# Decay attention and a two-layer network in one kernel: three edits to the order of the work between them

## The chip, the core and the metric

The kernel runs on one core of a Trainium2 chip. The metric is the device time of one execution in microseconds (us), as the median of several. A core has five engines, each with a queue of its own that it works off in order: TensorE (PE, matrix products; PEld loads its weights beside them), VectorE (DVE), ScalarE (ACT), GpSimd (POOL) and SyncE (SP), which here issues all the DMA transfers. Engines wait for each other and for transfers by semaphores. TensorE reads its operands from SBUF and writes to PSUM; ACT and DVE read both.

## The reference

```python
def _attn_ref(q, k, v, f):                      # B, H, S, D = 8, 8, 576, 64
    scores = scale * np.matmul(q, k.transpose(0, 1, 3, 2))
    cum = np.cumsum(np.log(np.clip(f, 0.0001, 1.0)), axis=-1)
    decay = cum[:, :, :, None] - cum[:, :, None, :]
    scores = np.where(causal, -1000000000.0, scores + decay)
    attn = np.exp(scores - np.max(scores, axis=-1, keepdims=True))
    attn = attn / (np.sum(attn, axis=-1, keepdims=True) + 1e-09)
    return np.matmul(attn, v)

def _moe_ref(x, w_in, w_out):                   # x: 4608 tokens x 512
    h = x @ w_in                                # 512 x 2048
    g = h * np.clip(h + 3.0, 0.0, 6.0) / 6.0
    return g @ w_out                            # 2048 x 512
```

The rows of x are the tokens: row (batch, position) holds the outputs of the 8 heads side by side, so a batch of 576 positions is 576 rows of x, and a row is complete when all 8 heads of its batch are done.

## The kernel before

**Units.** The list `VH` holds 68 attention units: four of kind A (the first 256 queries of two heads of batch 0 at once), eight of kind B (the other queries of batch 0, a head each) and 56 of kind F, the heads of batches 1 to 7. Their numbers are in the tiles' names: unit i has the score products `pn_i_0` and `pn_i_1` (two halves), the masked scores `pp`, the probabilities in two fp16 parts in a `ring` buffer, their transposed form `pT_i` (a DMA transpose, L666), the sums `pav` (probabilities times v, with a column of ones that gives the row sum), the row factors `rs`, and, for each pair of heads, `xf` and its fp16 parts `xhl`. Unit 12 is the first head of batch 1, unit 20 that of batch 2, and so on by eights.

**From attention to the two layers.** `x_move` (L736 on; the DMAs are L752) transposes a pair's `xhl` into `xT`, of which there are three, one for a tile of 512 tokens. The two-layer network runs by these nine tiles: 16 first-layer units (`ph_t_fc`, 12 products of 128x512 each, L778 to L780; then the clipping on ACT and DVE, L788 to L793, into `gT`) and four second-layer units (`po_t_s`, 48 products each, L800 to L802). The first products of a tile read the first pairs of heads; the 10th to 12th of `ph_t_0` read the last pair's part of `xT`. Tile 0 is done in two pieces, since its first 256 columns are there when the A units are.

**The order.** The loop over `VH` writes out, for each unit, its attention in steps, with eight calls of `fill(1)` between them. `fill` adds a rate to a credit and issues pieces of the two-layer work while the credit is at least 1; a piece costs 1.05 (half a first-layer unit) or 0.95 (six second-layer products), so a whole tile costs 64.0. The rate is `F_RATE[0]` in the B units, then `F_RATE[min(b, 2)]`: 0.6, 0.45 in batch 1, 1.02 from batch 2 on. `done(v)` puts a tile into the list `units` when the last head of its batch has been moved; it is called right behind `x_move`, in the middle of the second head of the next batch. What the loop writes is a priority: a list scheduler then places each instruction on its engine's queue, and may place one well ahead of where the loop wrote it.

**The weights.** `w_in` and `w_out` come as 64-bit floats (two 32-bit words each). For each of 16 chunks of each matrix `w_decode` makes fp32 of them (ACT L250, DVE L251 and L252, a sum of squares on ACT L256), and after the sum of a group `w_split` makes two fp16 parts (ACT L283; DVE L294, or, for three of the four groups of `w_in`, products with a scaled identity, `low`, L286 and L287). `w_step` does one step of this work; the loop calls it `wn` times for each unit, by `W_RATE` for A, B and F. Whatever is left when tile 0 reaches its second layer is written out there at once.

**v's power of two.** Each batch's v is scaled by a power of two, found from its largest element: the tile `vst` is loaded by three DMAs (`load_v`, L359 twice for a doubled first chunk, and L360 for the rest, about 1 MB), DVE takes the largest element by two reductions (L365, tile `vm`), a product with ones spreads it over the partitions (`pt_v`, L183), and a few DVE instructions write the scale to column `SV + b` of the tile `SC` and its inverse to `IV + b`. In batches 1 to 7 v is multiplied by it when it is split into fp16 parts (`v_split`, ACT L396, DVE L397). Batch 0 keeps v in fp32 as it is; there the scale joins the row factors: `rs` is the row sum plus a small number (L720), its reciprocal (L723), then times `SV` (L725), and L726 multiplies `pav` by it.

Of the kernel before, what the change touches and what calls it, by code (L numbers as in the profile page):

```python
# [15 lines left out]
ALU = mybir.AluOpType  # L16
# [4 lines left out]
def kernel(  # L21
# [10 lines left out]
    nc = tc.nc  # L32

    NHEAD, D, S = qk.shape
    D //= 2
    B = vS.shape[0]
    H = NHEAD // B
    NT, DM = out.shape
    DFF = w_in.shape[1]
    P = 128  # L40
# [5 lines left out]
    NFC = DFF // P  # L46
    TT = 512
# [3 lines left out]
    PSC = 2.0 ** 4  # L51
# [28 lines left out]
    )  # L80

    NQK, NL, NST = 3, 2, 3
    W_RATE = (8, 2, 4)
    H_COST = 1.05
    F_RATE = (0.6, 0.45, 1.02)
    PIN = 0
    PIN0 = 1
    LOW_W = 0
# [6 lines left out]
    QA = 256  # L95
# [104 lines left out]
    def scol(c):  # L200
        return SC[:, c:c + 1]
# [186 lines left out]
    def v_split(g):  # L388
        b, hp = divmod(g, NPAIR)
        t = v16[:, g % NV16]  # L390
        if g < NPAIR + NV16:
            nc.vector.memset(t[:, :, :, D:D + 1], 1.0)
        for j in range(2):
            o = (2 * hp + j) * (D + 1)
            src = vst[:, :, o:o + D]
            nc.scalar.activation(t[:, :, j, 0:D], src, AF.Copy, scale=scol(SV + b))  # L396
            nc.vector.scalar_tensor_tensor(  # L397
                t[:, :, j, D + 1:VW], src, scol(SV + b), t[:, :, j, 0:D],
                op0=ALU.mult, op1=ALU.subtract,
            )  # L400
# [278 lines left out]
    def av(v, ph):  # L679
        kind, n = VH[v]  # L680
        g = n if kind == "A" else n // 2
        b = g // NPAIR
        vt = v16[:, g % NV16]
        if kind == "F":
            jh = n % 2
            blk = [(n, c, c) for c in range(NCH)]
            vh, vl = vt[:, :, jh, 0:D + 1], vt[:, :, jh, D + 1:VW]
            for c in range(NCH):
                pb = ph[:, HT[c]:HT[c] + (2 * c + 1) * P].rearrange("p (g t) -> p g t", t=P)
                o1, o0 = pav[:, c, 0:D + 1], pav[:, c, 0:D]  # L690
                nc.tensor.matmul(o1, pb[:, c], vh[:, 0], start=True, stop=False)
                nc.tensor.matmul(o0, pb[:, c], vl[:, 0], start=False, stop=(c == 0))
                for k in range(1, c + 1):
                    nc.tensor.matmul(o1, pb[:, c + k], vh[:, k], start=False, stop=False)  # L694
                    nc.tensor.matmul(o0, pb[:, c + k], vl[:, k], start=False, stop=False)  # L695
                    nc.tensor.matmul(o1, pb[:, k - 1], vh[:, k], start=False, stop=(k == c))  # L696
        else:
            blk = blocks(v)
            for head, c, pl, m, js in blk:
                w0, _ = window(head)  # L700
                for jc, o, kk in js:
                    nc.tensor.matmul(
                        pav[:m, pl, :], ph[:kk, o:o + m], v_chunk(b, jc)[:kk, w0:w0 + NAV],
                        start=(jc == 0), stop=(jc == c),
                    )
        heads = sorted({x[0] for x in blk})
        if heads[0] % 2 == 0:
            xpair[g] = (
                p2.tile([P, NCH, P], F32, tag="xf", name=f"xf_{v}", bufs=1),
                p2.tile([P, NCH, 2, P], F16, tag="xhl", name=f"xhl_{v}", bufs=1),  # L710
            )
        xf, xhl = xpair[g]
        for head in heads:
            jh = head % 2
            mine = [x for x in blk if x[0] == head]
            p0, p1 = mine[0][2], mine[-1][2] + 1
            c0, c1 = mine[0][1], mine[-1][1] + 1
            vo = window(head)[1] if b == 0 else 0
            rs = p2.tile([P, NCH, 1], F32, tag="rs", name=f"rs_{v}_{jh}")[:, p0:p1]
            nc.vector.tensor_scalar(  # L720
                rs, pav[:, p0:p1, vo + D:vo + D + 1], PSC * 1e-9, None, op0=ALU.add
            )
            nc.vector.reciprocal(rs, rs)  # L723
            if b == 0:
                nc.vector.tensor_scalar(rs, rs, scol(SV + b), None, op0=ALU.mult)  # L725
            nc.vector.tensor_tensor(  # L726
                xf[:, c0:c1, jh * D:(jh + 1) * D], pav[:, p0:p1, vo:vo + D],
                rs.to_broadcast([P, p1 - p0, D]), op=ALU.mult,
            )
        if heads[-1] % 2:  # L730
            nc.scalar.copy(xhl[:, c0:c1, 0], xf[:, c0:c1])
            nc.vector.tensor_tensor(
                xhl[:, c0:c1, 1], xf[:, c0:c1], xhl[:, c0:c1, 0], op=ALU.subtract
            )

    def x_move(v):  # L736

        kind, n = VH[v]
        g = n if kind == "A" else n // 2
        b, cc = divmod(g, NPAIR)  # L740
        xhl = xpair[g][1]
        c0, c1 = {"A": (0, CA), "B": (CA, NCH), "F": (0, NCH)}[kind]

        if kind == "F":
            runs = [(0, 0, 1, 0), (0, 1, NCH, 1), (64, 1, NCH, 2)]
        else:
            runs = [(r * 64, c0, min(c1, NCH - r), r + 2 * c0) for r in range(2)]
        for r, c, last, u in runs:
            while c < last:
                t, q = divmod(S // 64 * b + u, TT // 64)  # L750
                k = min(last - c, (TT // 64 - q + 1) // 2)
                nc.sync.dma_start_transpose(  # L752
                    xT[t % 3][:, cc, q % 2, q // 2:q // 2 + k].rearrange("p c a t -> p (c a) t"),
                    xhl[r:r + 64, c:c + k].rearrange("p c a e -> p (c a e)"),
                )
                c += k
                u += 2 * k
# [115 lines left out]

    units = []

    credit, rates = [0.0], [1.0]

    def w_step():
        with tc.high_priority(offset=-LOW_W):
# [2 lines left out]
    def fill(k):  # L882
        credit[0] += k * rates[0]
        while credit[0] >= 1 and units:
            with tc.high_priority(offset=-LOW_M):
                r = next(units[0], 0)
            if r == 0:
                units.pop(0)
            else:
                credit[0] -= r  # L890
        credit[0] = min(credit[0], 1.0)

    def one(*a):
        yield from moe_tile(*a)

    def done(v):
        kind, n = VH[v]
        if kind == "A":
            if n == NPAIR - 1:
                units.append(one(0, 0, QA))  # L900
            return
        b, h = divmod(n, H)
        if h == H - 1:
            units.append(one(b, QA if b == 0 else 0, TT))
            if b == B - 1:
                units.append(one(B))

    prev = None
    pend_x = None
    vq = v_scale(0)  # L910
    for i, (kind, n) in enumerate(VH):
        b, h = divmod(n, H)
        if kind == "A":
            b = h = 0
        wn = W_RATE["ABF".index(kind)]
        rates[0] = F_RATE[0] if kind == "B" else F_RATE[min(b, 2)]
        ahead = i + 2 < NV
        if i + 3 < NV:
            load_x(i + 3)
        if ahead:  # L920
            load_c(i + 2)
        if b + 1 < B and h == 6:
            load_v(b + 1)
        if b and h % 2 == 1 and h < H - 1:
            v_split((n + 1) // 2)
        sg = rows(i) if kind == "F" else scores(i)
        front = ahead and VH[i + 2][0] != "F"
        next(sg)
        if i + 1 < NV:
            rests(i + 1)  # L930
        if ahead:
            parts(i + 2)
        fill(1)
        if b + 1 < B and h == 7:
            vq = v_scale(b + 1)
        next(vq, None)
        fill(1)
        ph = next(sg)
        if i + 1 < NV and VH[i + 1][0] != "F":
            max_rows(i + 1)  # L940
        for _ in range(wn // 2):
            w_step()
        fill(1)
        next(vq, None)
        next(sg, None)
        fill(1)
        if pend_x is not None:
            x_move(pend_x)
            done(pend_x)
            pend_x = None  # L950
        if front:
            natural(i + 2, 0)
        fill(1)
        if b + 1 < B and h == 7:
            for _ in vq:
                pass
            if b:
                v_split((n + 1) // 2)
        for _ in range(wn - wn // 2):
            w_step()  # L960
        next(sg, None)
        fill(1)
        if front:
            natural(i + 2, 1)
        fill(1)
        if prev is not None:
            av(*prev)
            if VH[prev[0]][0] == "A" or VH[prev[0]][1] % 2 == 1:
                pend_x = prev[0]
        if n == H:  # L970
            v_split(n // 2)
        fill(1)
        prev = (i, ph)
    rates[0] = 1.0
    av(*prev)
    fill(4)
    x_move(prev[0])
    done(prev[0])
    while units:
# [37 lines left out]
```

## Time and profile before

| | |
|---|---|
| median of 3 runs | 1086.47 us (1081.67 to 1088.14) |
| the profiled execution, its own time | 1084.35 us |
| its span, first to last instruction | 1082.6 us |
| mean granted TensorE clock | 0.986 of full speed |
| PE busy | 1012.2 us (94%) |
| DVE busy | 716.3 us (66%) |
| ACT busy | 610.3 us (56%) |
| POOL busy | 415.5 us (38%) |

A busy share is an average over stages: batch 0 and the weights until about 200 us, then batches 1 to 7 beside the tiles until about 890 us, then the last tiles alone. Matmuls are pipelined, so their busy times overlap. A line number stands for a line of the kernel before; of an instruction's tiles the profile leaves the numbers out.

### The profile page before, as it was taken

What the parts mean: (1) busy time and instruction counts of PE and PEld (TensorE: products, weight loads), DVE (VectorE), ACT (ScalarE), POOL (GpSimd) and SP (SyncE); (2) the same over time, 40 slices, a digit from 0 to 9 for tenths busy, and PEclk for the clock granted to TensorE, in tenths of its full rate; (3) what the DMA queues carried; (4) which work ended last, traced back from release to release, by engine and by line L of the source; (5) the groups of instructions that cost most, each with busy time, mean ns of one, the idle gap of its engine ahead of it and who ended that gap; (6) DMA issues with size and microseconds to landing.
All of it is one profiled execution on the core that took longest, in us unless ns stands there. A gap on an engine that the chain in (4) does not pass through costs nothing.

```text
span 1082.6 us, 20307 instructions
## 1 busy us (share of the span) xinstructions
PE 1012.2 (94%) x7074; PEld 578.3 (53%) x7074; DVE 716.3 (66%) x1903; ACT 610.3 (56%) x1285; POOL 415.5 (38%) x505
## 2 busy tenths in 40 slices
PE   2899977988999999989999989999999999999998
PEld 1667754755555555555554545555555555444443
DVE  7887889876885698477855795688668841510520
ACT  4786656755864577456744674477547841621520
POOL 7443454435434445444544444354445420000000
PEclk9999989999999999999999989999999999999999
DMA  8966447776756675666566856676666651000001
GB/s 244 295 196 212 117 104 136 156 151 133 164 109 143 141 146 122 134 144 142 124 139 123 160 112 130 137 168 120 129 139 129 105 110 48 1 10 30 1 1 39
DMA packets 261650, 133.74 MB, mean 124 GB/s; under 512 B 229444, under 2 KB 231036, under 8 KB 261548
## 3 DMA queue, kind: packets, MB, share of 16 engines
q1 hardware_dynamic: 261548, 132.45, 54.9%
q8 instruction: 56, 0.92, 0.4%
q14 instruction: 46, 0.38, 0.1%
HBM read 47.93 MB, written 9.73 MB: 53 GB/s over the span
## 4 chain that ended last, share of the span: by engine, by line
PE 73%; DVE 12%; DMA 5%; issue 3%; SPq 3%; POOL 2%; ACT 2%; DVEq 0%; POOLq 0%; ACTq 0%
PE po L801 11%; PE po L800 10%; PE po L802 10%; PE ph L778 9%; PE ph L779 9%; PE ph L780 9%; PE pn L611 3%; PE pn L608 3%; DMA vst<-in_vS_dram 2%; DVE pp L619 2%; SPq L752 2%; DVE ring L648 2%; PE pav L695 1%; PE pav L696 1%; PE pav L694 1%
## 5 line engine op out<-in xcount | busy, mean ns | idle before, releaser
L778 PE MATMUL ph<-xT,w 128*128 128x512 f16 (+1 forms) x640 | 230.7, 362 | 15.9 <-DVE r L791 10.4
L779 PE MATMUL ph<-xT,w 128*128 128x512 f16 (+1 forms) x640 | 228.9, 361 | 0.0
L780 PE MATMUL ph<-xT,w 128*128 128x512 f16 (+1 forms) x640 | 228.8, 361 | 0.0
L801 PE MATMUL po<-w,gT 128*128 128x512 f16 x576 | 217.1, 382 | 7.5 <-DVE w L294 7.5
L631 ACT ACTIVATE pp<-pp,nb 128x192 f32<-128x192 f32 x280 | 138.4, 552 | 143.7 <-DVE nb L625 143.6
L800 PE MATMUL po<-w,gT 128*128 128x512 f16 x576 | 214.5, 382 | 4.1 <-ACT w L283 2.2
L802 PE MATMUL po<-w,gT 128*128 128x512 f16 x576 | 216.9, 382 | 0.0
L648 DVE TENSOR_TENSOR ring<-pp,ring 128x128 f16<-128x128 f32 (+2 forms) x216 | 129.7, 615 | 84.6 <-ACT ring L645 83.6
L788 ACT ACTIVATE r<-ph,bias_r,SC 128x256 f32<-128x256 f32 (+7 forms) x272 | 144.4, 571 | 30.0 <-PE ph L780 25.9
L791 DVE SCALAR_TENSOR_TENSOR r<-r,ph 128x512 f32<-128x512 f32 (+1 forms) x160 | 100.0, 627 | 90.9 <-ACT r L788 90.8
L458 POOL TENSOR_TENSOR T<-ST,T 64x576 fp32r<-64x576 f32 (+1 forms) x68 | 99.7, 1466 | 139.0 <-DMA T<-TK 134.9
L619 DVE CUSTOM_DVE_ANT_0 pp<-pn,W 128x192 f32<-128x192 f32 x280 | 123.0, 481 | 19.3 <-PE pn L611 17.4
L793 DVE TENSOR_TENSOR gT<-r,gT 128x512 f16<-128x512 f32 (+1 forms) x160 | 114.0, 718 | 30.1 <-ACT gT L792 29.5
L792 ACT CAST gT<-r 128x512 f16<-128x512 f32 (+1 forms) x160 | 91.7, 574 | 73.4 <-DVE r L791 73.2
L608 PE MATMUL pn<-TK,TQ 68*128 68x192 f32 x336 | 125.1, 386 | 5.0 <-issue 4.0
L611 PE MATMUL pn<-T,T 128*128 128x192 f32 x336 | 113.9, 369 | 0.0
L645 ACT CAST ring<-pp 128x192 f16<-128x192 f32 x280 | 113.0, 452 | 0.0
L455 POOL TENSOR_TENSOR T<-ST,TQ 64x576 fp32r<-64x576 f32 (+2 forms) x68 | 97.5, 1433 | 22.5 <-PE pn L611 12.7
L654 POOL TENSOR_TENSOR ring<-pp,ring 128x128 f16<-128x128 f32 x96 | 62.5, 651 | 106.9 <-ACT ring L645 77.7
L779 PEld LDWEIGHTS <-w 128*128 128x128 f16 x640 | 62.5, 98 | 66.2 <-issue 20.7
L802 PEld LDWEIGHTS <-gT 128*128 128x128 f16 x576 | 57.0, 99 | 76.2 <-issue 15.1
L778 PEld LDWEIGHTS <-w 128*128 128x128 f16 x640 | 62.9, 98 | 61.9 <-issue 13.7
(136 smaller groups left out, 1715.2 us busy)
## 6 DMA issues: line engine op xcount, KB each, us to landing
ST<-in_qk_dram SPq DMA_DIRECT2D x64, 288.0 KB
T<-TK SPq DMA_DIRECT2D x64, 144.0 KB
out_dram<-o SPq DMA_DIRECT2D x36, 256.0 KB
ring<-in_w_out_dram SPq DMA_DIRECT2D x16, 512.0 KB
T<-TQ SPq DMA_DIRECT2D x56, 144.0 KB
vst<-in_vS_dram SPq DMA_DIRECT2D x7, 1040.0 KB
ring<-in_w_in_dram SPq DMA_DIRECT2D x9, 512.0 KB
w<-in_w_in_dram SPq DMA_DIRECT2D x7, 512.0 KB
```

What stands on the lines that cost most here:

```text
L608: nc.tensor.matmul(dst, TQ[i][0:D + 4, qs], TK[i][0:D + 4, a:e], start=True, stop=False)
L611: nc.tensor.matmul(dst, T7[j][:, qs], T1[j][:, a:e], start=False, stop=True)
L619: nc.vector.tensor_tensor_reduce(pp[:r, w:w + kw], pn[:r, o:o + kw], W[:r, 4 * P + r - kw:4 * P + r], 1.0, -3.0e38, ALU.add, ALU.max, accu ...
L631: nc.scalar.activation(x_, x_, AF.Exp, bias=nb[:r, e0 + x:e0 + x + 1], scale=0.125)
L648: eng.tensor_tensor(hl[:r, a:a + c * P], pp[:r, at[c] + 64:at[c] + kw], hl[:r, h0[c] + 64:h0[c] + kw], op=ALU.subtract,)
L778: nc.tensor.matmul(ph, w1[0][:, cc, fs_], xh, start=(cc == 0), stop=False)
L779: nc.tensor.matmul(ph, w1[0][:, cc, fs_], xl, start=False, stop=False)
L780: nc.tensor.matmul(ph, w1[1][:, cc, fs_], xh, start=False, stop=(cc == NCC - 1))
L788: nc.scalar.activation(r[:, a:e], ph[:, a:e], AF.Relu, bias=bias_r, scale=scol(A1 + NG * b + fc * NG // NFC))
L800: nc.tensor.matmul(po, gT[:, 0, fc, ts_], w2[:, fc, 0, :], start=(fc == 0), stop=False)
L801: nc.tensor.matmul(po, gT[:, 0, fc, ts_], w2[:, fc, 1, :], start=False, stop=False)
L802: nc.tensor.matmul(po, gT[:, 1, fc, ts_], w2[:, fc, 0, :], start=False, stop=(fc == NFC - 1))
```

## The change

Three edits. **First**, in the B units the loop calls `w_step` five times for each unit, where it was two (`W_RATE`). **Second**, in batch 0 the first instruction of `rs` multiplies the row sum by the inverse scale, `IV`, in the same instruction that adds the small number, and the third instruction is gone. **Third**, from batch 2 on the rate isn't a constant: `even(h)` takes what is left in the list (counted in `left`), less a reserve of 8, and divides it evenly over the eight `fill`s of each head that remains before the next tile can join; and `done` of an F pair is called not right behind `x_move` but at the start of the next head.

```diff
-    W_RATE = (8, 2, 4)
+    W_RATE = (8, 5, 4)
-    F_RATE = (0.6, 0.45, 1.02)
+    F_RATE = (0.6, 0.45)
...
-            nc.vector.tensor_scalar(
-                rs, pav[:, p0:p1, vo + D:vo + D + 1], PSC * 1e-9, None, op0=ALU.add
-            )
+            total = pav[:, p0:p1, vo + D:vo + D + 1]
+            if b == 0:
+                nc.vector.tensor_scalar(
+                    rs, total, PSC * 1e-9, scol(IV + b), op0=ALU.add, op1=ALU.mult
+                )
+            else:
+                nc.vector.tensor_scalar(rs, total, PSC * 1e-9, None, op0=ALU.add)
             nc.vector.reciprocal(rs, rs)
-            if b == 0:
-                nc.vector.tensor_scalar(rs, rs, scol(SV + b), None, op0=ALU.mult)
...
+    credit, rates, left = [0.0], [1.0], [0.0]
+    TILE = NFC * 2 * H_COST + TT // P * NFC // 2 * (2.0 - H_COST)
+    RESERVE = 8.0
+    def queue(unit, columns):
+        units.append(unit)
+        left[0] += TILE * columns / TT
+    def even(h):
+        heads = (1 - h) % H + 1
+        return min(max((left[0] - RESERVE) / (8 * heads), 0.5), 1.25)
...
-        rates[0] = F_RATE[0] if kind == "B" else F_RATE[min(b, 2)]
+        if moved is not None:
+            done(moved)
+            moved = None
+        rates[0] = F_RATE[0] if kind == "B" else F_RATE[b] if b < 2 else even(h)
...
         if pend_x is not None:
             x_move(pend_x)
-            done(pend_x)
+            if VH[pend_x][0] == "F":
+                moved = pend_x
+            else:
+                done(pend_x)
             pend_x = None
```

The scheduler turns this into other places on the queues. SyncE's queue where the last pair of batch 3 (`xhl_34`) is moved into tile 3, before: the outputs of tile 2 (`o_2_3` is its last) are sent before the fifth transpose.

```order
L812 DMA out_0_dram<-o_2_2_5605 128x512
L411 DMA ST2_105<-in_qk_dram 128x576
L666 DMA_TRANSPOSE pT_36_5553<-ring1_124 128x12x128
L752 DMA_TRANSPOSE xT0_117<-xhl_34_5539 128x2x64
L752 DMA_TRANSPOSE xT0_117<-xhl_34_5539 128x4x64
L752 DMA_TRANSPOSE xT1_118<-xhl_34_5539 128x4x64
L752 DMA_TRANSPOSE xT0_117<-xhl_34_5539 128x4x64
L812 DMA out_0_dram<-o_2_3_5752 128x512
L752 DMA_TRANSPOSE xT1_118<-xhl_34_5539 128x4x64
```

And now, from the second of these transposes on:

```order
L755 DMA_TRANSPOSE xT0_117<-xhl_34_5431 128x4x64
L755 DMA_TRANSPOSE xT1_118<-xhl_34_5431 128x4x64
L755 DMA_TRANSPOSE xT0_117<-xhl_34_5431 128x4x64
L815 DMA out_0_dram<-o_2_1_5632 128x512
L755 DMA_TRANSPOSE xT1_118<-xhl_34_5431 128x4x64
L417 DMA TK1_97<-decay_dram 2x576
L666 DMA_TRANSPOSE pT_37_5601<-ring2_125 128x13x128
L666 DMA_TRANSPOSE pT_37_5601<-ring0_123 128x12x128
L419 DMA TQ1_94<-decay_dram 2x576
L453 DMA T71_102<-TQ0_93 64x576
L454 DMA T11_100<-TK0_96 64x576
L815 DMA out_0_dram<-o_2_2_5761 128x512
```

The pair is moved while tile 2 has its third and fourth output blocks (`o_2_2`, `o_2_3`) still ahead of it; before, its last block was done by then.

SyncE's queue where batch 5's v is loaded, before: both kinds of load stand behind the transposes of unit 38.

```order
L666 DMA_TRANSPOSE pT_38_5874<-ring1_124 128x13x128
L411 DMA ST1_104<-in_qk_dram 128x576
L666 DMA_TRANSPOSE pT_38_5874<-ring2_125 128x12x128
L359 DMA vst_112<-in_vS_dram 64x520 x2
L360 DMA vst_112<-in_vS_dram 128x4x520
```

And now: the two L359 stand where they were, behind unit 38, and L360 behind the transposes of unit 39.

```order
L417 DMA TK0_96<-decay_dram 2x576
L666 DMA_TRANSPOSE pT_39_5923<-ring0_123 128x13x128
L419 DMA TQ0_93<-decay_dram 2x576
L453 DMA T71_102<-TQ2_95 64x576
L454 DMA T11_100<-TK2_98 64x576
L666 DMA_TRANSPOSE pT_39_5923<-ring1_124 128x12x128
L360 DMA vst_112<-in_vS_dram 128x4x520
```

The load has moved back by a head, and no L359 stands right ahead of it any more. VectorE's queue around the reductions of the same v (`vm5`), before, with the first-layer instructions `r_3_...` of tile 3:

```order
L791 SCALAR_TENSOR_TENSOR r_3_6_0_6093<-r_3_6_0_6093,ph_3_6_0_6080 128x512
L619 ISA pp_39_1_6120,MF1_109<-pn_39_1_6115,W_88 128x320
L619 ISA MF1_109 128x1
L619 ISA pp_39_1_6120,MF1_109<-pn_39_1_6115,W_88 128x448
L619 ISA MF1_109 128x1
L365 TENSOR_REDUCE vm5_6776<-vst_112 128x1 x2
L648 TENSOR_TENSOR ring0_123<-pp_39_0_6066,ring0_123 128x128
L625 TENSOR_SCALAR nb_39_6056<-MF1_109 128x2
L793 TENSOR_TENSOR gT_116<-r_3_6_0_6093,gT_116 128x512
L648 TENSOR_TENSOR ring0_123<-pp_39_0_6066,ring0_123 128x512
L791 SCALAR_TENSOR_TENSOR r_3_7_0_6132<-r_3_7_0_6132,ph_3_7_0_6108 128x512
```

And now:

```order
L794 SCALAR_TENSOR_TENSOR r_3_3_0_6096<-r_3_3_0_6096,ph_3_3_0_6037 128x512
L625 TENSOR_SCALAR nb_40_6106<-MF0_108 128x3
L796 TENSOR_TENSOR gT_116<-r_3_3_0_6096,gT_116 128x512
L619 ISA pp_40_1_6171,MF0_108<-pn_40_1_6166,W_88 128x320
L619 ISA MF0_108 128x1
L619 ISA pp_40_1_6171,MF0_108<-pn_40_1_6166,W_88 128x448
L619 ISA MF0_108 128x1
L365 TENSOR_REDUCE vm5_6673<-vst_112 128x1 x2
L794 SCALAR_TENSOR_TENSOR r_3_4_0_6144<-r_3_4_0_6144,ph_3_4_0_6131 128x512
```

The reductions come a head later too, between the products 3 and 4 of tile 3 and no longer between 6 and 7, and the next `r` follows them directly.

More of the change, by code (lines that the diff above doesn't have):

```diff
@@ L874 @@
     units = []
-    credit, rates = [0.0], [1.0]
+    credit, rates, left = [0.0], [1.0], [0.0]
[7 more added lines that the diff above has]
+        return min(max((left[0] - RESERVE) / (8 * heads), 0.5), 1.25)
     def w_step():
@@ L890, in fill @@
                 credit[0] -= r
+                left[0] -= r
         credit[0] = min(credit[0], 1.0)
@@ L899, in done @@
             if n == NPAIR - 1:
-                units.append(one(0, 0, QA))
+                queue(one(0, 0, QA), QA)
             return
@@ L903, in done @@
         if h == H - 1:
-            units.append(one(b, QA if b == 0 else 0, TT))
+            queue(one(b, QA if b == 0 else 0, TT), TT - QA if b == 0 else TT)
             if b == B - 1:
-                units.append(one(B))
+                queue(one(B), TT)
     prev = None
-    pend_x = None
+    pend_x = moved = None
     vq = v_scale(0)
@@ L976 @@
     fill(4)
+    if moved is not None:
+        done(moved)
     x_move(prev[0])
```

## Prediction

> **What bounds the kernel now.** I read the page first: TensorE is busy for 94% of the span, no other engine for more than 66%, and its clock stays near full. Then the same by stages, cut where tiles begin (columns: busy time and instructions of each engine, granted clock, share and rate of the DMA engines).
>
> ```profile
> PE 1012.2 (94%) x7074; PEld 578.3 (53%) x7074; DVE 716.3 (66%) x1903; ACT 610.3 (56%) x1285; POOL 415.5 (38%) x505
> ...
> 36.00:196.00 160.00, 139.03 (x973) 100.25 (x973) 138.15 (x407) 111.17 (x235) 75.61 (x78) 0.95 0.64 165
> 196.00:300.00 104.00, 96.83 (x800) 62.78 (x798) 81.41 (x221) 67.65 (x153) 44.20 (x54) 0.97 0.70 154
> ...
> 366.80:809.30 442.50, 428.71 (x3210) 237.04 (x3210) 319.11 (x844) 266.25 (x576) 207.39 (x256) 0.99 0.66 136
> 809.30:1082.60 273.30, 268.83 (x1545) 130.49 (x1544) 108.63 (x231) 112.33 (x216) 35.67 (x43) 1.00 0.22 47
> ```
>
> The kernel ends when TensorE has done all its products; the change removes none, so only idle PE time and time at a lowered clock can be won. There are three stages. From 36 to 196 us, with batch 0 and the weights, PE is idle for 21 us, and DVE, with 138.15 of 160 us, is as full as PE. From 366.8 to 809.3, four whole tiles, PE is idle for 13.8 us. Behind 809.3 it is idle for 4.5 us and nothing in the change touches it. So the waits of the third row decide, and those that DVE causes in the first:
>
> ```profile
> PE ph L778 <- DVE r L791: 8.8, 5, 4.5
> PE ph L778 <- DMA xT<-xhl: 5.3, 2, 2.7
> ...
> PE po L801 <- DVE w L294: 7.5, 4, 4.7
> PE pn L608 <- issue: 4.0, 2, 2.9
> PE po L800 <- ACT w L283: 2.2, 2, 1.8
> ```
>
> (Total, times, longest; the first two are all the PE waits between 300 and 900 us, the others are of 36 to 196 us.)
>
> **The boundary of a batch.** The two waits for `xT` are the first products of tiles 3 and 4 that need the last pair. In each, PE runs out of the old tile while SyncE still issues transposes:
>
> ```profile
> 474.68 5.03 SPq L752 DMA_TRANSPOSE xT<-xhl  x4
> ...
> 480.37 1.18 SPq L752 DMA_TRANSPOSE xT<-xhl  x1
> ...
> 480.95 0.38 PE L778 MATMUL ph<-xT,w 128*128 128x512 f16 x1 [2.71 <-DMA xT<-xhl]
> ...
> 592.42 0.38 PE L778 MATMUL ph<-xT,w 128*128 128x512 f16 x1 [2.60 <-DMA xT<-xhl]
> ...
> 481.30:484.80 3.50, 3.50 (x31) 2.34 (x28) 1.58 (x6) 2.15 (x4) 0.35 (x1) 0.51 0.74 152
> 592.40:596.00 3.60, 3.58 (x45) 2.56 (x45) 1.93 (x7) 2.24 (x5) 0.40 (x1) 1.00 1.04 139
> ```
>
> The transposes take 6 us to issue. By the order, two second-layer blocks of the old tile, `o_2_2` and `o_2_3`, now stand behind the move: at most 2 x 48 products at about 0.21 us (the last stage holds one each 0.2 us: 1545 in 268.83, some of them short), some 20 us, and at least half of it if the first block is nearly through. That covers 6 us and the 2.7 beyond them, so both waits go: **5.3 us**. Behind the first, the clock row shows 0.51 for 3.5 us, so 1.7 us of full-speed work was lost; behind the second it shows 1.00. That goes too: **7.0 us** in all. The cover is those two blocks; if it were gone, the 7.0 would be back, and at worst 2.7 more at each of the three other boundaries of the row (8 us). Calling `done` later costs nothing by itself, as `fill` issues the old tile's pieces meanwhile.
>
> The Trainium skill ("TensorE: Matmul & The Clock Gate", section "Why this matters for your kernels") puts the limit at idle gaps of about 3 us before the clock is halved. The trace differs, since the clock fell behind 2.71 us of idle; by the page the term would be 5.3 and not 7.0.
>
> **v's load, which the diff doesn't touch.** The other PE waits, 8.8 us, follow DVE's wait for `vst`:
>
> ```profile
> 724.52 1.52 SPq L359 DMA_DIRECT2D vst<-in_vS_dram  x2
> 726.10 0.58 SPq L360 DMA_DIRECT2D vst<-in_vS_dram  x1
> ...
> 731.79 1.75 DVE L365 TENSOR_REDUCE vm<-vst 128x1 f32<-128x1536 f32 x1 [2.22 <-DMA vst<-in_vS_dram]
> ...
> 627.24 0.58 PE L778 MATMUL ph<-xT,w 128*128 128x512 f16 x1 [4.50 <-DVE r L791]
> ...
> 627.24:631.60 4.36, 4.36 (x11) 1.57 (x11) 4.33 (x15) 3.15 (x7) 1.11 (x2) 0.51 0.95 180
> ...
> L648 DVE TENSOR_TENSOR ring<-pp,ring 128x128 f16<-128x128 f32 (+3 forms) x128 | 79.1, 635 | 55.5 <-ACT ring L645 55.0
> ...
> L793 DVE TENSOR_TENSOR gT<-r,gT 128x512 f16<-128x512 f32 x64 | 50.5, 794 | 5.2 <-ACT gT L792 5.0
> L791 DVE SCALAR_TENSOR_TENSOR r<-r,ph 128x512 f32<-128x512 f32 x64 | 43.5, 679 | 10.1 <-ACT r L788 10.1
> L397 DVE SCALAR_TENSOR_TENSOR v<-vst,SC,v 128x320 f16<-128x320 f32 x32 | 19.4, 624 | 0.1
> L732 DVE TENSOR_TENSOR xhl<-xf,xhl 128x640 f16<-128x640 f32 x16 | 14.2, 890 | 4.7 <-ACT xhl L731 4.6
> L625 DVE TENSOR_SCALAR nb<-MF 128x2 f32<-128x2 f32 x64 | 20.1, 315 | 1.2
> ```
>
> Load and reductions both move back by one head, behind unit 39 for 38. Ahead of the load, the two L359 no longer stand in the way: 1.5 us sooner. Ahead of the reductions, an even unit for an odd one, DVE has no `xhl` (0.89), no L397 (0.62), one `r` and one `gT` fewer (0.68 and 0.79): 3.0 us less. So the wait for `vst` grows by 1.5 us. Against that the next `r` now follows the reductions directly, where two `ring`, an `nb` and a `gT` stood between, at least 2.3 us by their rows (635, 315 and 794 ns), while ahead of the reductions an `nb` and a `gT` were added between `r` and them, about 1 us. For PE, which waits from `r` to `r`, that is 1.5 - 2.3 + 1.0 = +0.2 us, and I take **0**. The bounds: all of it goes (8.8, and 2.2 for the 4.36 us at 0.51), or each of the five boundaries pays what the worst paid.
>
> **The row factors of batch 0.** Sixteen L725 go, and sixteen L720 get a second operation and `IV` as an operand.
>
> ```profile
> L725 DVE TENSOR_SCALAR rs<-rs,SC x16: 206/366/1218, 42.4 to 145.9; 128x2 f32<-128x2 f32 x8, 128x3 f32<-128x3 f32 x8
> ...
> L720 DVE TENSOR_SCALAR rs<-pav x72: 137/156/167, 29.9 to 901.9; 128x5 f32<-128x5 f32 x56, 128x2 f32<-128x2 f32 x8, 128x3 f32<-128x3 f32 x8
> ...
> L725 DVE TENSOR_SCALAR rs<-rs,SC 128x2 f32<-128x2 f32 (+1 forms) x16 | 8.4, 526 | 0.2
> ...
> 76.48 1.90 POOL L458 TENSOR_TENSOR T<-ST,T 64x576 fp32r<-64x576 f32 x1 [5.60 <-DMA T<-TK]
> ...
> 77.31 1.10 DVE L725 TENSOR_SCALAR rs<-rs,SC 128x3 f32<-128x3 f32 x1
> ```
>
> L725 takes 206 ns at best and up to 1218, and the long one at 77.31 ends at 78.41, with POOL's L458 (78.38): it waited that instruction out. L720, which reads PSUM, never took over 167 ns in 72. If the joined instruction behaves like L725, what goes is an L720 each, 16 x 0.156 = 2.5 us; if like L720, all of L725, 8.4 us. It reads its tensor from PSUM, so I take 8.4. The "GPSIMD Engine Reference" of the Trainium skill, section "Key points", says that GpSimd contends with those DVE instructions that run in a two-port mode or have two SBUF inputs, which the joined one has not; that is the 8.4.
>
> How much of it reaches the end? DVE itself is idle for 160 - 138.15 = 21.85 us of that stage, waiting for PE and ACT, so time freed is partly spent on waiting; what reaches the PE waits there (13.7 us in the three rows) I put at half: **4 us**, between 0 and 8.4.
>
> **The weights.** Five steps for two moves the decoding and splitting of `w_out` forward; no instruction goes. On a DVE that is full for 86% of the stage, a piece that comes sooner puts another back. I take **0**. The bounds: the waits for `w_out`'s parts go, 7.5 + 2.2 = 9.7 us; or the B heads, which now share DVE with more weight work, come later by what the steps take that are pulled ahead. The same waits stand for that: as much again, 9.7, is the other end.
>
> **The even rate** of 1.0 (a tile of 64 over 64 `fill`s) for 1.02 changes nothing where PE is full: the old rate issued 65.3 for 64.0 and so came out empty once a batch; that is the wait priced above.
>
> **The sum.** Against the profiled execution's own time, 1084.35 (span 1082.6): 1084.35 - 7.0 - 4 = 1073.35; the scheduler's other moves in the stages before 300 us, where PE is idle for 7.2 us behind 196, I count at -1: **1072 us**. The profiled execution lies 2.1 us below the median of the three runs, inside their range; I leave that out. About 1% is what a measurement of this kernel can tell from no change: 10.9 us, so 1075.6 and 1097.3 are the limits.
>
> **The rivals.**
>
> *DVE's freed time is all spent on waiting.* Only the boundary pays: 1084.35 - 7.0 = 1077.4. For it: DVE's 21.85 us of idle time beside its load. Against it: PE's longest waits there are for DVE.
>
> *The weights do come sooner in effect.* The 9.7 us go as well: 1072 - 9.7 = 1062. For it: the waits name `w`'s parts. Against it: DVE is as full as before.
>
> *v's load becomes the wait of every boundary, slower than before.* L360 now stands right behind unit 39's transposes, which wait for DVE; the reductions stand 1.5 us nearer. If the load lands as late as at 622 us at each of five boundaries, each costs 4.5 + 2.2 us: 33.5 for the 11.0 of now, 22.5 more. 1072 + 22.5 = 1094.5. It decides from about 12 us on, that is if each boundary's PE wait grows to over 4 us. Against it: the same four boundaries with the load 3.5 us ahead of the point where DVE was ready (726.10 to 731.79 - 2.22) cost 1.3 each.
>
> *The boundary isn't relieved*, since the scheduler puts the pieces elsewhere: 1084.35 - 4 = 1080. Against it: SyncE's order shows two blocks behind the move.
>
> **How the numbers follow.** Forecast, 1066 to 1080 around 1072: 0.50. Only the boundary: 0.20. Weights: 0.13. v's load: 0.11. Not relieved: 0.06. Of the forecast, three quarters and more lie below 1075.6, so faster: 0.40 + 0.13 + a little of the second case, 0.56; slower needs more than the v rival gives, 1097.3: 0.05; the rest, 0.39, within 1%. The range takes in the first three cases and part of the others, 1061 to 1086.
>
> **What would show it.** No PE wait for `xT` from tile 2 on, and no clock at 0.51 behind one. The joined instruction at 140 to 170 ns, never longer. DVE waits for `vst` of 3 to 5 us, and PE waits for `r` of about 9 us in all between 300 and 900. PE's waits for L294 shorter by some 4 us together. I am wrong if PE waits at boundaries for `vst` by more than 4 us each, or if PE's idle time from 36 to 196 us grows beyond 21 us.

## The result and the profile after

The change is slower: **1099.3 us** in the median of four runs (1093.32 to 1100.81) against 1086.59 before. The ratio is 1.0129, with a 95% interval of 1.009 to 1.0168. The profiled execution took 1099.5 us, its span 1097.7.

The page of the kernel after (span; busy time, share and instructions of each engine), and its stages in the columns of the prediction's first fence:

```profile
span 1097.7 us, 20288 instructions
...
PE 1013.1 (92%) x7074; PEld 578.9 (53%) x7074; DVE 730.9 (67%) x1887; ACT 610.1 (56%) x1285; POOL 409.8 (37%) x505
```

```profile
36.00:196.00 160.00, 135.86 (x985) 100.46 (x985) 140.13 (x389) 111.78 (x238) 73.67 (x76) 0.95 0.62 161
196.00:300.00 104.00, 93.66 (x817) 61.45 (x815) 84.40 (x225) 66.00 (x148) 47.25 (x57) 0.98 0.73 160
300.00:900.00 600.00, 575.58 (x4327) 317.56 (x4326) 434.56 (x1130) 357.66 (x775) 264.43 (x332) 0.98 0.63 130
```

The kernel before from 300 to 900 us, in the same columns:

```profile
300.00:900.00 600.00, 585.83 (x4397) 323.15 (x4395) 425.49 (x1137) 358.56 (x774) 270.72 (x335) 0.99 0.64 131
```

PE is busy as long as before (1013.1 for 1012.2 us), so the time went into idle PE: 84.6 us of the span for 70.4, 14.2 of the 15.1 us by which the span grew. By stage the idle time went from 21.0 to 24.1 us between 36 and 196, from 7.2 to 10.3 up to 300, and **from 14.2 to 24.4 between 300 and 900** (ahead of 36 us it fell by 2.3). The last is the largest part, and there it has one name. PE's waits of the kernel after, from 300 to 900 us (total, times, longest):

```profile
PE ph L781 <- DVE r L794: 20.9, 6, 6.8
PE pav L691 <- DMA pT<-ring: 2.2, 5, 0.8
PE pn L611 <- POOL T L458: 1.3, 1, 1.3
```

The 5.3 us for `xT` are gone. The 8.8 us for `r` have become 20.9. DVE and SyncE's queue around one of these waits in the kernel after (start, duration, instruction; in brackets the idle time before it and what ended it), first SyncE, then DVE, then PE and the clock behind it:

```profile
380.10 1.53 SPq L359 DMA_DIRECT2D vst<-in_vS_dram  x2
381.72 0.54 SPq L815 DMA_DIRECT2D out_dram<-o  x1
382.35 7.40 SPq L755 DMA_TRANSPOSE xT<-xhl  x5
389.86 0.38 SPq L417 DMA_DIRECT2D TK<-decay_dram  x1
390.35 1.28 SPq L666 DMA_TRANSPOSE pT<-ring  x1
391.68 0.93 SPq L419 DMA_DIRECT2D TQ<-decay_dram  x1
392.71 0.49 SPq L453 DMA_DIRECT2D T<-TQ  x1
393.25 0.59 SPq L454 DMA_DIRECT2D T<-TK  x1
393.94 1.51 SPq L666 DMA_TRANSPOSE pT<-ring  x1
395.51 1.10 SPq L360 DMA_DIRECT2D vst<-in_vS_dram  x1
```

```profile
389.33 0.67 DVE L794 SCALAR_TENSOR_TENSOR r<-r,ph 128x512 f32<-128x512 f32 x1
...
392.64 0.62 DVE L619 CUSTOM_DVE_ANT_0 pp<-pn,W 128x448 f32<-128x448 f32 x1
393.19 0.08 DVE L619 DVE_READ_ACCUMULATOR2_ANT MF<- 128x1 f32 x1
401.76 2.88 DVE L365 TENSOR_REDUCE vm<-vst 128x1 f32<-128x1536 f32 x2 [8.49 <-DMA vst<-in_vS_dram]
404.56 0.68 DVE L794 SCALAR_TENSOR_TENSOR r<-r,ph 128x512 f32<-128x512 f32 x1
...
405.29 0.59 PE L781 MATMUL ph<-xT,w 128*128 128x512 f16 x1 [6.12 <-DVE r L794]
...
405.29:408.20 2.91, 2.91 (x9) 1.42 (x9) 2.91 (x10) 2.91 (x6) 0.02 (x1) 0.51 0.60 133
```

The same load in the kernel before:

```profile
389.34 1.66 SPq L359 DMA_DIRECT2D vst<-in_vS_dram  x2
391.05 0.58 SPq L360 DMA_DIRECT2D vst<-in_vS_dram  x1
...
393.31 0.67 DVE L791 SCALAR_TENSOR_TENSOR r<-r,ph 128x512 f32<-128x512 f32 x1
...
397.03 2.88 DVE L365 TENSOR_REDUCE vm<-vst 128x1 f32<-128x1536 f32 x2 [2.10 <-DMA vst<-in_vS_dram]
...
401.30 0.68 DVE L791 SCALAR_TENSOR_TENSOR r<-r,ph 128x512 f32<-128x512 f32 x1
...
402.04 0.38 PE L778 MATMUL ph<-xT,w 128*128 128x512 f16 x1 [1.29 <-DVE r L791]
```

What counts is the **lead** of the load: how long after L360's issue DVE comes to the reductions (their start, less their wait, less the issue). Before it is 397.03 - 2.10 - 391.05 = 3.88 us. After, L360 is issued 15.4 us behind the first L359, since an output, five transposes of a pair and the next unit's transposes and other transfers stand between; DVE is at the reductions 2.24 us before L360 is even issued. From its issue to the reductions the load takes about as long in both (5.98 and 6.25 us). So DVE stands for 8.49 us, and everything queued behind the reductions with it, the next `r` first; PE, whose next product belongs to a first-layer unit that needs this `r`, stands for 6.12, and gets half the clock behind it (0.51 in the last row). The four boundaries, from the same two rows of each:

| v of batch | before: lead, DVE waits, PE waits | after: lead, DVE waits, PE waits |
|---|---|---|
| 4 | 3.88, 2.10, 1.29 | -2.24, 8.49, 6.12 |
| 5 | 3.18, 3.86, 1.31 | 0.33, 7.00, 5.94 |
| 6 | 1.74, 5.03, 4.50 | -1.83, 7.24, 6.76 |
| 7 | 3.47, 2.22, 1.32 | 1.31, 5.08, 1.42 |

### The profile page after: what moved, and what is told of

Same layout as the page of the kernel before. It is cut to its first block, busy times and chain, and to the rows that moved or that the text cites. A ratio compares the mean times of both kernels' runs of the same rounds, so it can differ in the third digit from the quotient of the medians.

```text
span 1097.7 us, 20288 instructions
## 1 busy us (share of the span) xinstructions
PE 1013.1 (92%) x7074; PEld 578.9 (53%) x7074; DVE 730.9 (67%) x1887; ACT 610.1 (56%) x1285; POOL 409.8 (37%) x505
## 4 chain that ended last, share of the span: by engine, by line
PE 65%; DVE 11%; DMA 9%; ACT 5%; issue 5%; POOL 3%; SPq 2%; DVEq 0%; POOLq 0%; ACTq 0%
PE po L803 10%; PE po L804 10%; PE po L805 10%; PE ph L781 8%; PE ph L782 8%; PE ph L783 8%; DMA vst<-in_vS_dram 4%; PE pn L611 3%; PE pn L608 3%; DVE pp L619 2%; ACT pp L631 2%; DVE ring L648 1%; DMA pT<-ring 1%; DMA TQ<-mr 1%; DVE vm L365 1%
## 5 line engine op out<-in xcount | busy, mean ns | idle before, releaser
L804 PE MATMUL po<-w,gT 128*128 128x512 f16 x576 | 214.4, 381 | 6.0 <-DVE w L294 6.0
L805 PE MATMUL po<-w,gT 128*128 128x512 f16 x576 | 214.1, 380 | 0.0
L803 PE MATMUL po<-w,gT 128*128 128x512 f16 x576 | 211.7, 380 | 1.2 <-ACT o L814 0.8
L648 DVE TENSOR_TENSOR ring<-pp,ring 128x128 f16<-128x128 f32 (+2 forms) x216 | 138.1, 648 | 69.4 <-ACT ring L645 68.8
L796 DVE TENSOR_TENSOR gT<-r,gT 128x512 f16<-128x512 f32 (+1 forms) x160 | 119.4, 748 | 29.5 <-ACT gT L795 28.5
L608 PE MATMUL pn<-TK,TQ 68*128 68x192 f32 x336 | 127.7, 392 | 6.0 <-issue 5.0
L611 PE MATMUL pn<-T,T 128*128 128x192 f32 x336 | 116.7, 376 | 7.1 <-POOL T L458 7.1
L645 ACT CAST ring<-pp 128x192 f16<-128x192 f32 x280 | 115.5, 451 | 0.3 <-DMA pT<-ring 0.3
L782 PEld LDWEIGHTS <-w 128*128 128x128 f16 x640 | 63.1, 99 | 80.8 <-issue 32.0
L783 PEld LDWEIGHTS <-w 128*128 128x128 f16 x640 | 63.2, 99 | 65.7 <-issue 9.0
L781 PEld LDWEIGHTS <-w 128*128 128x128 f16 x640 | 62.4, 99 | 58.9 <-issue 11.1
```

Of the source, the lines that this page charges most:

```text
L608: nc.tensor.matmul(dst, TQ[i][0:D + 4, qs], TK[i][0:D + 4, a:e], start=True, stop=False)
L611: nc.tensor.matmul(dst, T7[j][:, qs], T1[j][:, a:e], start=False, stop=True)
L648: eng.tensor_tensor(hl[:r, a:a + c * P], pp[:r, at[c] + 64:at[c] + kw], hl[:r, h0[c] + 64:h0[c] + kw], op=ALU.subtract,)
L781: nc.tensor.matmul(ph, w1[0][:, cc, fs_], xh, start=(cc == 0), stop=False)
L782: nc.tensor.matmul(ph, w1[0][:, cc, fs_], xl, start=False, stop=False)
L783: nc.tensor.matmul(ph, w1[1][:, cc, fs_], xh, start=False, stop=(cc == NCC - 1))
```

## The experiments

Theory 1: the loss is v's load, whose lead the third edit takes away. Theory 2: the loss lies in batch 0 and the weights, where PE's idle time has also grown. Each kernel was timed in five rounds; the kernel before had a median of 1083.79 us beside the first four, 1083.3 beside the next four and 1083.46 beside the last four. A ratio is to the kernel before timed beside it (it isn't quite the quotient of the two medians).

### Each edit alone, and the change with the reductions held

```diff
e1_weights (kernel before):    -W_RATE = (8, 2, 4)
                               +W_RATE = (8, 5, 4)
e2_row_factor (kernel before): the edit of rs, as in the change
e3_boundary (kernel before):   even(), queue() and the later done(), as in the change
e4_late_reduction (changed kernel), in v_scale, with late[v] = the reciprocal of unit v's rs
                               and i the unit that writes the reductions out:
+    with tc.issue_after(late[i - 2]):
         nc.vector.tensor_reduce(pm[:, i:i + 1], ...)
```

> The kernel before with the first edit alone (five weight steps for each B unit). Theory 1 (the loss is the load of v at the batch boundaries, which the third edit brings about): 1082 to 1090, and the boundary waits of PE from 300 to 900 us stay at some 9 us for r and 5 us for xT. Theory 2 (the loss comes from batch 0 and the weights, where PE's idle time grew from 6.2 to 10.4 us between 36 us and the first head of batch 1): 1090 to 1096.

> The kernel before with the second edit alone (the scale in the row sum's instruction). Theory 1: 1080 to 1087, with boundary waits as before. Theory 2: above 1088. My prediction's term for this edit was 4 us off 1086, 0 to 8.4.

> The kernel before with the third edit alone (even rate, the tile queued at the next head). Theory 1: the whole loss is here: 1093 to 1101; DVE waits for vst by 5 to 8.5 us and PE for r by 5 to 7 us at the boundaries, since L360 stands behind the transposes of the next unit. Theory 2: 1077 to 1083, the gain that the prediction gave the boundary.

> The changed kernel with the two reductions of v's largest element held on DVE until the reciprocal of the row factors of the unit two before the one that writes them out (some 30 us later than now); the load stays where it is. Theory 1: the boundary waits of PE for r (20.2 us in four of them, and 10 to 12 us of lowered clock behind) go: 1070 to 1080. Theory 2: DVE has other work to wait with, and the time stays above 1092.

| | us | ratio, 95% |
|---|---|---|
| e1, weights alone | 1089.38 | 1.0057, 1.0031 to 1.0083 |
| e2, row factor alone | 1085.58 | 1.0022, 0.9996 to 1.0047 |
| e3, boundary alone | 1097.3 | 1.0132, 1.0105 to 1.0159 |
| e4, change, reductions held | 1075.69 | 0.9937, 0.9913 to 0.996 |

The third edit alone costs as much as the whole change. Its waits of PE from 300 to 900 us:

```profile
PE ph L778 <- DVE r L791: 17.7, 5, 7.2
PE pav L691 <- DMA pT<-ring: 2.9, 4, 1.2
PE pn L611 <- POOL T L458: 0.5, 1, 0.5
PE pt_v L183 <- DVE r L791: 0.2, 1, 0.2
```

And with the reductions held, in e4 (its stage row below the waits):

```profile
PE pav L694 <- DMA pT<-ring: 2.9, 2, 2.7
PE pn L614 <- POOL T L461: 1.4, 1, 1.4
PE pt_v L183 <- DVE vm L374: 0.5, 1, 0.5
...
300.00:900.00 600.00, 595.77 (x4459) 327.13 (x4460) 440.44 (x1136) 360.62 (x777) 264.99 (x336) 1.00 0.64 132
```

Not one wait for `r` is left, the stage's idle time is 4.2 us for 24.4, and the kernel is 23.6 us faster than the change in another series of runs (1099.3 to 1075.69). Load, rates and weights are as in the change; only DVE gets to the reductions later (at the four boundaries by 10 to 26 us of the span), when the load has long landed. Theory 1 stands. Theory 2 has a small share: e1 loses about 6 us. Its profile has PE idle for 15.0 us from 36 to 196, 6 less than before, but 9.2 from 196 to 300, at a lower clock, and attention's waits for `pT` there. Over the whole span PE is idle for 3.6 us less than before (66.8 for 70.4) but busy for 9.4 more (1021.6 for 1012.2), at a mean granted clock of 0.978 for 0.986: what e1 loses shows as lowered clock, not as idle time.

```profile
36.00:196.00 160.00, 145.01 (x970) 102.60 (x969) 142.97 (x405) 111.11 (x236) 78.42 (x77) 0.94 0.59 160
196.00:300.00 104.00, 94.82 (x785) 60.21 (x783) 80.78 (x214) 64.92 (x147) 41.77 (x49) 0.93 0.72 154
...
PE pav L691 <- DMA pT<-ring: 6.6, 3, 4.3
```

### Is it the load's place? And what is the boundary edit worth without the wait?

```diff
e5_before_late:   the kernel before, with the reductions held as in e4
e6_boundary_late: e3 with the reductions held as in e4
e7_load_first (changed kernel):
-            load_v(b + 1)
+            with tc.high_priority(offset=2000):
+                load_v(b + 1)
e8_defer_alone (kernel before): done() of an F pair at the start of the next head; rate 1.02 as before
```

> The kernel before with the two reductions of v's largest element held on DVE as in the run before this one, and nothing of the change. If the wait for v's load also costs the kernel before what its profile shows (8.8 us of PE waits for r and some 3.4 us at half clock behind): 8 to 12 us below the kernel before. If DVE is only waited for elsewhere instead: within 4 us of it.

> The third edit alone, with the reductions held. Against the run with the reductions held and none of the change this shows what the third edit is worth when v's load can't be waited for: by the prediction's term 5 to 7 us less (both xT waits gone); by the rival (those waits are covered or replaced anyway) the same within 2 us.

> The whole change, with the three loads of v at a higher priority for the scheduler, so that L360 stands right behind the two L359, a unit earlier than now, and the reductions follow them by a unit as in the kernel before. If the place of L360 on SyncE's queue made the loss: DVE's waits for vst at 2 to 5 us, and a time within 6 us of the kernel before. If it is the reductions that came earlier, whatever the load does: waits of 5 us and more, and 1093 or above.

> The kernel before with only the later queueing of a tile (at the start of the next head), at the old constant rate. One second-layer block (o_2_3) now stands behind the pair's move, 48 products or some 10 us, and L360 stays where it was. If one block covers the transposes: no xT wait at the boundaries and 3 to 7 us below the kernel before. If it does not: as the kernel before within 3 us.

| | us | ratio, 95% |
|---|---|---|
| e5, before, reductions held | 1078.54 | 0.9952, 0.9926 to 0.9978 |
| e6, boundary edit, reductions held | 1081.67 | 0.9975, 0.9952 to 0.9998 |
| e7, change, v's load first | 1094.13 | 1.0081, 1.0058 to 1.0103 |
| e8, later queueing alone | 1089.01 | 1.0038, 1.0016 to 1.0059 |

**e7** was to put L360 back and did, but the reductions moved forward with it, by about a unit:

```profile
383.32 1.30 SPq L359 DMA_DIRECT2D vst<-in_vS_dram  x2
384.68 0.58 SPq L360 DMA_DIRECT2D vst<-in_vS_dram  x1
...
390.83 2.88 DVE L365 TENSOR_REDUCE vm<-vst 128x1 f32<-128x1536 f32 x2 [7.62 <-DMA vst<-in_vS_dram]
...
PE ph L781 <- DVE r L794: 13.0, 4, 5.2
```

Its lead is 390.83 - 7.62 - 384.68 = -1.47 us here and 1.77, -0.96 and 4.75 at the next three; the waits are 7.62, 4.52, 7.48 and 1.99. So the first arm of its expectation fell, and the time is that of the second: it isn't the place of L360 as such, but the distance of the two, and an earlier load alone doesn't lengthen it.

**e8** lost the waits for `xT` too (one block covers the transposes), with L360 where it was, but was slower, by some 4 us (its profiled execution took 1091.76 us for a median of 1089.01): the leads at the four boundaries are 2.55, 1.79, 3.44 and 0.15 us, 7.9 in all for 12.3 before, and PE waits for `r` by 13.0 us from 300 to 900. That is 1.1 us less than the waits for `r` and `xT` of before together, but each of the four at the boundaries (3.38, 3.43, 2.13 and 3.07 us) has 3.5 us at a granted clock of 0.50 to 0.57 behind it. In the kernel before only the longest of its four has that (4.50 us, then 0.50); behind the three of 1.3 us the clock is 1.00. The even rate without the later queueing wasn't run, so their shares in e3 aren't known.

**e5 and e6** answer what the boundary edit is worth when nobody waits for v: nothing; e6 is the slower by 3 us, though the intervals overlap. Both paid a new wait of 3.8 us at 140 us, for batch 1's scale, whose reductions were held too. The last four runs take that out.

### With the stages ahead left alone

```diff
e9_hold3:        the kernel before, reductions held for the v of batches 3 to 7 only
e10_even3:       the kernel before, even rate and later queueing, the rate from batch 3 on
                 +    F_RATE = (0.6, 0.45, 1.02)
                 +    rates[0] = ... F_RATE[b] if b < 3 else even(h)
e11_even3_hold3: e10, reductions held as in e9
e12_change_hold3: the changed kernel, reductions held as in e9
```

> The kernel before with the reductions held from batch 3's v on, so that its queues are those of the kernel before up to about 250 us. By the waits shown: PE's waits for r behind v's loads (8.4 us of 8.8 lie there) and 3.4 to 5 us at half clock go: 8 to 13 us below the kernel before. If the gain of the earlier run with held reductions came from batches 1 and 2: within 4 us of the kernel before.

> The kernel before with the even rate and the later queueing from batch 3 on alone; its queues are those of the kernel before up to about 230 us. If the whole loss is the load of v: 8 to 15 us above the kernel before, with 15 us and more of PE waits for r between 300 and 900 us. If a part of the loss came from the even rate in batch 2 and the stages ahead: within 5 us of it.

> Both: even rate and later queueing from batch 3 on, and the reductions held from batch 3's v on. If the boundary term of the prediction holds once v's load is out of the way: 5 to 7 us below the run with held reductions alone (1064 to 1072). If the waits for xT are only replaced: the same within 2 us.

> The whole change with the reductions held from batch 3's v on (before, they were held in all batches: 1075.7). If holding them in batches 1 and 2 cost the 3.7 us wait seen at 142 us: 1070 to 1074. If not: 1074 to 1079. Against the run with the even rate and the held reductions alone it shows what the first two edits are worth beside them: by the prediction 4 us less, by the runs of each edit alone 2 to 8 us more.

| | us | ratio, 95% |
|---|---|---|
| e9, before, held from batch 3 | 1073.45 | 0.9911, 0.988 to 0.9941 |
| e10, even rate from batch 3 | 1100.1 | 1.0155, 1.0121 to 1.0188 |
| e11, both | 1076.3 | 0.994, 0.9919 to 0.9961 |
| e12, change, held from batch 3 | 1074.8 | 0.9921, 0.9893 to 0.995 |

The same twenty-odd us again, from one pair of instructions: e10 against e11. The stage and PE's waits from 300 to 900 us, e9 first, then e11:

```profile
300.00:900.00 600.00, 594.52 (x4492) 327.84 (x4491) 434.70 (x1134) 359.73 (x775) 268.86 (x334) 1.00 0.64 132
...
PE ph L781 <- DMA xT<-xhl: 5.5, 4, 2.4
```

```profile
300.00:900.00 600.00, 593.08 (x4442) 325.77 (x4439) 446.53 (x1132) 357.71 (x771) 264.24 (x333) 1.00 0.63 131
...
PE pav L694 <- DMA pT<-ring: 4.2, 5, 1.8
PE pt_v L183 <- DVE nb L628: 1.7, 1, 1.7
PE pn L614 <- POOL T L461: 0.6, 1, 0.6
PE ph L781 <- DVE r L794: 0.2, 1, 0.2
```

The even rate does take away the 5.5 us for `xT`, and 6.7 us of other waits come in their place; DVE is busy for 11.8 us more. Why attention's transposes then come later wasn't tried. e9, e11, e12 and e4 lie within 3 us, with overlapping intervals: once the reductions are held, none of the three edits is worth anything that these runs can tell. **The best version measured is e9**, the kernel before with DVE's reductions moved back, 1073.45 us.

## Why the prediction was wrong, by its steps

**v's load, "I take 0": the step that failed.** The right place was named, and its rival (v's load as the wait of every boundary, 1094.5 us) is what happened, but it had a chance of 0.11. In the last four runs holding the reductions gains 23.8 us with the even rate from batch 3 on (e10 to e11) and 10.0 without it (e9), so the edit made v's load dearer by some 14 us where the sum had 0. Three of the step's numbers were off.

- *"Load and reductions both move back by one head", and the load 1.5 us sooner relative to its queue.* On SyncE only the two L359 were counted as what L360 no longer stands behind. What came to stand in front of it wasn't: an output, five transposes of 7.40 us, two of the next unit, and four other transfers. At the first boundary, counted from the first L359, L360 came 13.7 us later than before (15.4 for 1.7) and DVE's arrival only 7.6 (13.2 for 5.6). The lead shrank by 6.1, 2.9, 3.6 and 2.2 us, 3.7 in the mean, where 1.5 was forecast.
- *From `r` to `r`, +0.2 us.* In the rows above it went from 401.30 - 393.31 = 8.0 to 404.56 - 389.33 = 15.2 us: 6.4 for the longer wait; ahead of the reductions +2.3 (1.0 forecast; DVE also waited for ACT and PE there); behind them -1.5 (-2.3 forecast).
- *The bound.* The rival priced a boundary at 4.5 us of PE; three of the four cost 5.9 to 6.8.

The rival's text already had L360 "right behind unit 39's transposes, which wait for DVE". The place was right; the reason wasn't. From L815 to L360 took 13.8, 12.7, 13.6 and 10.7 us at the four boundaries, and of that SyncE waited for other engines for 1.6, 1.4, 1.0 and 0.8 us in all. The rest is issuing, as the SyncE rows above show for the first, one issue right behind the other. So in the change the load stood behind 11 to 14 us of its own queue, and the step priced none of it. e7, where the load stands ahead of those issues, shows that this place alone isn't the cause, since there the reductions came sooner too; why the scheduler puts them so close behind the load stays open. Both signs that the prediction named for being wrong came: three of the four boundaries cost PE more than 4 us each, and its idle time from 36 to 196 us was 24.1, over 21.

**The boundary, -7.0.** Right as to the waits: from 300 to 900 us there is no wait for `xT` in the kernel after, e3, e8 and e11. Wrong as to their worth: e5 to e6 and e9 to e11 moved by +3.1 and +2.9 us, not by -7. A wait of PE that goes is worth its length only if no other comes up in its place; in e11 6.7 us did for 5.5. The prediction's rivals had this for DVE's freed time, not for this term.

**The row factors, -4.** The price of the instruction nearly held: it reads PSUM and took 223 ns at most, where L725 took up to 1218; its 198 to 223 ns lie above the 140 to 170 that the prediction named. The kernel after, batch 0's form (times in ns, shortest, median, longest):

```profile
L723 DVE TENSOR_SCALAR rs<-pav,SC x16: 198/209/223, 34.5 to 148.6; 128x2 f32<-128x2 f32 x8, 128x3 f32<-128x3 f32 x8
```

That is 0.05 us above the L720 of before, and L725's 8.4 us are gone; but e2 isn't faster. In its profile and that of the change PE takes a product with ones of the weights' scale, `pt_w`, and waits for it where the kernel before waited 0.4 us (from 36 to 196 us, e2 and then the change):

```profile
PE pt_w L183 <- ACT w L288: 3.3, 1, 3.3
```

```profile
PE pt_w L183 <- ACT w L288: 3.8, 1, 3.8
```

DVE's freed time didn't reach the end, as the first rival had it. Why this wait comes up isn't shown, and e2's profiled execution took 1092.53 us, 7 us over its median.

**The weights, 0 within 9.7.** e1 cost about 6 us, inside the bounds, and the case "the weights do come sooner in effect" was half true: the idle time did fall by 6 us in their stage, and was lost again to a lower clock, most of all behind it (0.93 for 0.97 from 196 to 300 us). **The scheduler's other moves, -1,** can't be told from these two: in the change's profile PE's idle time between 36 and 300 us grew by 6.3 us for all three together.

## What to carry to other kernels

When an order moves a transfer and the instruction that waits for it, price the *lead*: the time from the transfer's issue to the waiting engine's arrival, with everything that now stands ahead of the issue on its queue, and compare it with how long the transfer takes. An instruction whose result nobody needs yet (`pt_v` of the v above runs 42 us behind the reductions, at 443.4 us) doesn't belong at the place where its operand might just have landed, on an engine that everyone waits for: holding two reductions back was worth 10 us here, and three edits with good arguments nothing. And one wait that is removed on a full engine is worth its length only after looking at what would be late next.

## What the runs showed of the hardware

How long the granted clock stays down differs from wait to wait. In the change PE waited 3.76 us up to 49.2 us and 2.83 us up to 56.5, and from 49.6 to 63.4 us the clock was 0.51. Behind the single waits of the prediction's rows it was 0.51 for 3.5 us (2.71 us) and for 4.4 us (4.50 us), and behind one of 2.60 us it didn't fall. That the two waits add up because they are close may be so by this one place, but no run was made for it.

```profile
49.60:63.40 13.80, 10.44 (x34) 7.44 (x35) 8.31 (x32) 9.75 (x21) 3.75 (x4) 0.51 0.73 211
```

The load of 1 MB took 5.4 to 7.3 us from its issue to the reductions at the eight places of the table, no longer after than before in the mean; the wait grew with the lost lead, not with the load. And a transpose holds SyncE's queue: the 148 of L755 in the kernel after took 1.25 us each to issue in the median, 1.16 at least.
